# A hand-ordered attention and MLP kernel on one core: a new timetable, the second x tile on another queue, a shorter warm-up

## The chip, the cores and the metric

The kernel runs on one core of a Trainium2 chip. The metric is the device time of one execution in microseconds (us). The engines are named as in the profile: PE (TensorE, matmuls), PEld (its weight loads, which overlap PE), DVE (VectorE), ACT (ScalarE), POOL (GpSimd) and SP (SyncE, which issues nearly all DMAs here).

## The reference

One transformer block over 2048 tokens of width 576: layernorm, attention with 32 heads of 18 in four segments of 512 tokens with a running memory between segments, a residual, layernorm, an MLP with 4608 hidden units and tanh gelu, a residual.

```python
for s in range(N):                       # N = 4 segments of L = 512
    logits = einsum('bhqd,bhkd->bhqk', qs, ks) * scale + mask     # causal inside the segment
    a_dot = einsum('bhqk,bhkd->bhqd', softmax(logits), vs)
    pq = phi(qs)                         # phi(t) = t + 1 if t > 0 else exp(t)
    a_mem = einsum('bhld,bhde->bhle', pq, M) / (einsum('bhld,bhd->bhl', pq, z)[..., None] + 1e-06)
    outs.append(g * a_mem + (1.0 - g) * a_dot)     # g = sigmoid(beta), one per head
    pk = phi(ks); M = M + einsum('bhld,bhle->bhde', pk, vs); z = z + pk.sum over l
h = x + concat(outs) @ wo                # q, k, v = layernorm(x) @ wq, wk, wv
h2 = h + gelu(layernorm(h) @ w1 + b1) @ w2 + b2
```

## The kernel before

The work is cut into some 1840 small steps (`Op`), each on one engine. Each has a tag and a name: `X` is layernorm of x (`stats`, `rstd`, `apply`) with its transposes (`TX`), `P` the projections, `A` attention, `M` the memory's update, `B` output projection, residual and second layernorm, `C` the MLP's first matmul (`F1`) with its evictions (`copy`) and gelu, `D` the second (`F2`) with the last addition (`oadd`). The digit is the segment; in segment 0 a second digit tells its halves or tiles apart. A step's number counts from 0: `A01mask` has four.

The order is written out by hand in `TIMETABLE`: for each step the engine (letters `p a d g s` for PE, ACT, DVE, POOL, SP) and its place among all steps. `Graph.add` looks a step up there, and `Graph.schedule` sorts the steps by place and, with costs of its own, picks the buffer of each. Each engine then runs its steps in that order; between engines, semaphores make a step wait for its inputs and buffers. So a place moves a step past others of its engine, never ahead of its data. SP's order is the order in which DMAs are issued, and a DMA that has to wait holds up those behind it.

The start. `warm_up` issues matmuls on zeros (`warm`): four, four, then two, then X00's first transposes, then three. The first 128 rows of x come in two pieces, `dma.0` on SP's queue and `x0b` on ACT's; the second 128 rows are `x1`, on ACT's queue behind `x0b`. Next on SP stand the two halves of the k weights; then x's fourth tile, the q weights, x's third tile, held until x's first piece has landed (`gate`), and the v weights. In segment 0 the first two tiles are projected by `proj2` (ten matmuls of 288 columns each for k and for q, P00Pk and P00Pq), the rest by `proj_pair`, in two steps (`P`, `R`, between which a `pass` changes banks) or fused in one. q and k rows go to DRAM (`qkst`) and come back transposed (`A0flip`, `A1flip` and so on). The head gates come from beta, a small DMA (`dma.4`) behind P00's `qkst`; `gates.0` on ACT turns it into an exponential, ahead of the first exponential of the scores (`A00exp.0`).

Attention runs by steps: scores on PE (`st0`, `st`), `exp` on ACT over 128x2048, a causal `mask` on DVE (a product with `tri`) or POOL (an affine select), the product with v on PE (`val`), then `valT`, `rec`, `comb` and `oT` on DVE or POOL; for later segments also the memory's part (`eg`, `rg`, `pq`, `mem`, `memT`, `memfin`). The output projection of segment 0 is B00 and B01 (rows 0 to 255), B02 and B03. PE fills its time with the projections of the next segment and with F1 and F2 of the one before. w1 comes in nine groups per segment through four buffers (`C00dma` and so on), w2 in six chunks that stay (`W2dma`); the last three chunks lie where the buffers of q and k rows were (`to_w2`).

Of the kernel before, what the change touches and what calls it, by code (L numbers as in the profile page):

```python
# [25 lines left out]
    "A00exp": "a 91 124",  # L26
    "A00mask": "g101 d125 g133 g164",
    "A00st0": "p 80 109",
    "A01comb": "d172 g197 d225 g214",
    "A01exp": "a 134 136 161 153",  # L30
    "A01mask": "g145 d147 g182 d195",
    "A01oT": "d 198 240 245 234 246",
    "A01rec": "d 168 186 224 212",
    "A01st0": "p 129 132 155 143",
    "A01swap": "g241 d242",
    "A01val": "p 151 201",
    "A01valT": "d 157 158 211 210",
    "A02comb": "g 317 392",
    "A02exp": "a 191 228 207 266 272 283 312",
    "A02mask": "g219 g254 g267 d337",  # L40
    "A02rec": "d 288 369",
    "A02st0": "p 187 222 204 239 271 282 301",
    "A02val": "p 280 281 342 344",
    "A02valT": "d 287 352",
    "A03comb": "g 422 464",
    "A03exp": "a 338 364 350 394 399 420 428",
    "A03mask": "g378 g360 g397 d439",
    "A03oT": "d 381 419 425 485 492",
    "A03rec": "d 417 463",
    "A03st0": "p 332 362 339 379 398 411 427",  # L50
    "A03swap": "a480 g470",
    "A03val": "p 409 412 454 455",
    "A03valT": "d 414 460",
    "A0flip": "s 95 87 128 137 184 189 260 313",
    "A1comb": "g592 d631 g702 g780 g806 g854 d843 g862",
    "A1comb2": "g611 g686 d709 d792 g808 d855 d846 g874",
    "A1eg": "a 462 421 530 677 583 740 719 801",
    "A1exp": "a 458 498 479 579 557 587 613 626 650 674 690 727 713 735 766 750 799 810 817 786",
    "A1flip": "s 410 401 450 575 449 556 688 705",
    "A1mask": "d494 g527 g502 g546 d555 g598 g596 d590 g616 g662 g627 g639 g628 g691 g710 g707 d730 g753 g745 g717 g759 d743 g774 d782 g762 g818 g800 d812 "  # L60
        "g811 g836 g787 g820",
    "A1mem": "p 503 504 629 716 732 815 795 832",
    "A1memT": "d 515 505 630 724 736 824 796 848",
    "A1memfin": "g602 g652 g666 d756 g775 g838 g834 g865",
    "A1oT": "d 822 890 859 876 899",
    "A1pq": "d 477 465 574 703 712 779 755 802",
    "A1rec": "d 584 605 657 741 768 837 797 849",
    "A1rec2": "d 566 606 694 763 784 845 842 853",
    "A1rg": "g 456 407 521 670 497 754 752 788",
    "A1st": "p 457 487 478 570 544 586 600 625 644 665 683 725 711 734 765 749 794 809 816 778",  # L70
    "A1swap": "a 875 885",
    "A1val": "p 563 599 679 726 764 789 826 851",
    "A1valT": "d 565 604 687 729 771 798 839 852",
    "A2comb": "d933 g1009 d1052 d1050 g1120 d1132 g1206 g1219",
    "A2comb2": "d991 g1010 g1061 d1095 d1166 d1142 d1217 g1223",
    "A2eg": "a 823 841 880 1001 971 1040 1129 1060",
    "A2exp": "a 872 840 879 857 893 977 983 967 1020 1028 1042 1059 1071 1049 1083 1107 1119 1148 1128 1161",
    "A2flip": "s 728 807 833 863 888 998 1043 896",
    "A2mask": "g883 d882 g881 g886 g955 g903 d909 g894 g1012 d1014 d1019 g987 g990 d1022 d1029 g1033 g1056 d1077 g1072 d1085 g1087 d1110 g1102 g1084 g1111 "
        "d1133 g1150 d1156 g1186 g1173 g1201 g1195",  # L80
    "A2mem": "p 878 901 994 1045 1003 1118 1160 1162",
    "A2memT": "d 889 902 1008 1062 1016 1125 1168 1167",
    "A2memfin": "g973 g935 g1051 d1074 g1070 g1138 d1216 g1183",
    "A2oT": "d 1090 1105 1204 1227 1236",
    "A2pq": "d 861 884 919 1015 974 1063 1152 1097",
    "A2rec": "d 897 912 1018 1064 1027 1131 1191 1174",
    "A2rec2": "d 929 992 1041 1038 1108 1124 1198 1215",
    "A2rg": "g 844 850 892 941 918 1013 1065 1048",
    "A2st": "p 868 827 877 856 891 976 982 954 1006 1023 1031 1057 1068 1047 1078 1091 1113 1139 1127 1155",
    "A2swap": "a 1225 1229",  # L90
    "A2val": "p 905 970 1032 1036 1096 1117 1158 1211",
    "A2valT": "d 915 972 1034 1037 1098 1123 1169 1214",
    "A3comb": "g1340 g1338 g1405 d1399 g1516 g1474 g1559 g1544",
    "A3comb2": "g1347 g1348 g1408 g1404 g1531 d1493 g1566 g1560",
    "A3eg": "a 1220 1193 1308 1294 1353 1376 1470 1427",
    "A3exp": "a 1185 1210 1222 1298 1232 1328 1342 1309 1371 1356 1416 1394 1420 1436 1446 1457 1468 1479 1487 1499",
    "A3flip": "s 1146 1187 1255 1165 1145 1300 1414 1357",
    "A3mask": "g1271 g1256 g1273 g1251 g1260 g1310 d1272 d1243 d1358 g1362 d1344 g1336 g1329 d1383 d1374 g1364 d1438 g1453 d1437 g1421 g1458 g1443 d1448 "
        "d1447 d1481 d1504 g1502 d1529 d1521 g1488 g1519 g1501",
    "A3mem": "p 1283 1269 1368 1350 1425 1461 1537 1530",  # L100
    "A3memT": "d 1297 1303 1382 1352 1426 1462 1541 1546",
    "A3memfin": "d1343 d1324 g1386 d1389 d1518 d1471 d1558 d1549",
    "A3oT": "d 1372 1429 1569 1568 1575",
    "A3pq": "d 1252 1242 1335 1317 1381 1423 1472 1492",
    "A3rec": "d 1307 1304 1385 1375 1430 1463 1550 1547",
    "A3rec2": "d 1339 1331 1403 1398 1473 1465 1555 1543",
    "A3rg": "g 1208 1240 1320 1314 1261 1387 1415 1486",
    "A3st": "p 1184 1209 1213 1288 1230 1327 1337 1302 1370 1354 1410 1392 1419 1434 1445 1452 1467 1478 1485 1498",
    "A3swap": "d 1570 1565",
    "A3val": "p 1306 1311 1390 1391 1454 1459 1532 1533",  # L110
    "A3valT": "d 1316 1318 1402 1397 1455 1464 1536 1538",
    "B00Po": "p 247",
    "B00Ro": "p 255",
    "B00T": "p 305 328",
    "B00apply": "d 289",
    "B00copy": "d 310 329",
    "B00dma": "s 233 507",
    "B00hadd": "d 259 263",
    "B00pass": "d 250",
    "B00rstd": "g 268",  # L120
    "B00stats": "d 265",
    "B00tail": "d 290",
    "B01Po": "p 256",
    "B01Ro": "p 270",
    "B01T": "p 324 326",
    "B01apply": "d 304",
    "B01copy": "d 325 327",
    "B01dma": "s 235 847",
    "B01hadd": "d 273 276",
    "B01pass": "d 257",  # L130
    "B01rstd": "g 285",
    "B01stats": "d 284",
    "B01tail": "g 316",
    "B02Po": "p 510",
    "B02Ro": "p 519",
    "B02apply": "d 640",
    "B02dma": "s 461 858 673",
    "B02hadd": "d 520 526",
    "B02pass": "d 513",
    "B02rstd": "g 622",  # L140
    "B02stats": "d 541",
    "B02tail": "d 648",
    "B03Po": "p 576",
    "B03Ro": "p 585",
    "B03apply": "d 612",
    "B03dma": "s 501 829 672",
    "B03flip": "s 692 700",
    "B03hadd": "d 591 595",
    "B03pass": "g 578",
    "B03rstd": "g 608",  # L150
    "B03stats": "d 603",
    "B03tail": "d 618",
    "B1Po": "p 906 922 907 916",
    "B1Ro": "p 920 926 927 925",
    "B1apply": "d 948 993 975 958",
    "B1dma": "s 860 949 980 951 1039 999 937 1207 997 910 1092 966",
    "B1flip": "s 1079 1094",
    "B1hadd": "d 921 924 953 968 938 939 928 930",
    "B1pass": "g914 d923 g908 d917",
    "B1rstd": "g 942 986 969 950",  # L160
    "B1stats": "d 931 985 940 932",
    "B1tail": "g957 d995 g984 d963",
    "B2Po": "p 1312 1249 1246 1237",
    "B2Ro": "p 1319 1254 1253 1262",
    "B2apply": "d 1395 1360 1296 1315",
    "B2dma": "s 1321 1365 1400 1205 1359 1366 1163 1287 1346 1284 1599 1388",
    "B2flip": "s 1422 1428",
    "B2hadd": "d 1323 1326 1265 1275 1257 1258 1285 1286",
    "B2pass": "g 1313 1250 1247 1241",
    "B2rstd": "g 1341 1277 1264 1299",  # L170
    "B2stats": "d 1332 1276 1263 1293",
    "B2tail": "d1396 g1361 g1325 g1363",
    "B3Po": "p 1602 1594 1584 1580",
    "B3Ro": "p 1613 1603 1588 1585",
    "B3apply": "d 1675 1677 1637 1652",
    "B3dma": "s 1612 1721 1679 1604 1655 1685 1573 1611 1646 1557 1628 1676",
    "B3flip": "s 1686 1707",
    "B3hadd": "d 1645 1653 1609 1640 1597 1608 1587 1593",
    "B3pass": "d1605 g1601 g1586 g1581",
# [148 lines left out]
    "omg": "g 152",  # L328
    "ones": "a 262 192",
    "tri": "g 55",  # L330
    "warm": "p 1 2 3 23",
    "x0b": "a 8",
    "x1": "a 10",
}
# [1214 lines left out]
```

## Time and profile before

| what | value |
|---|---|
| median of 3 runs | 445.64 us (445.15 to 446.35) |
| the profiled execution | 446.14 us |
| its span | 444.4 us |
| PE busy | 433.7 us |
| ACT busy | 298.1 us |
| DVE busy | 286.3 us |
| POOL busy | 179.5 us |
| DMA | 76.26 MB, mean 172 GB/s |

The span is shorter than the device time of the same execution, because what lies before the first and after the last instruction is left out of it. Busy times of several engines overlap. A matmul's end is modelled, so a busy PE is not a PE at its peak. "Idle before" is time in which an engine had nothing running, with what released it.

### The profile page before, as it was taken

To read this page: it belongs to the slowest core of one execution; us is meant where nothing else is said; L and a number is where in the kernel's file an instruction comes from. 1 tells how busy PE (TensorE), PEld (TensorE's weight loads), DVE (VectorE), ACT (ScalarE), POOL (GpSimd) and SP (SyncE) were. 2 spreads that over 40 slices of the span, in tenths; PEclk is the share of its full clock that TensorE was granted. 3 is DMA by queue.
4 is the path that set the end of the run, shared out by engine and by line. 5 is a ranking of instruction groups with operands and counts; after the bars stand their busy time and mean duration, and the time that the engine had idled before them with its cause. 6 is when DMAs were issued, how large, how long until landed. Compare 5 with 4: busy or idle time off the path is not lost.

```text
span 444.4 us, 12086 instructions
## 1 busy us (share of the span) xinstructions
PE 433.7 (98%) x5089; PEld 277.8 (63%) x5089; DVE 286.3 (64%) x635; ACT 298.1 (67%) x274; POOL 179.5 (40%) x321
## 2 busy tenths in 40 slices
PE   8978999999999999999999999999999999999997
PEld 4755677776677676664444766654457775446775
DVE  4899988899778998968788888642875410000011
ACT  3799889999878898776799976675855001565000
POOL 4587657356735765834132765412111400110000
DMA  7599989997999955893783236913634357550110
GB/s 283 167 217 258 257 251 283 251 287 203 191 270 333 286 118 175 175 236 94 162 228 91 73 90 193 232 20 133 219 97 165 90 142 133 172 177 1 40 41 29
DMA packets 81591, 76.26 MB, mean 172 GB/s; under 512 B 59008, under 2 KB 68864, under 8 KB 81536
## 3 DMA queue, kind: packets, MB, share of 16 engines
q1 hardware_dynamic: 81248, 75.23, 63.5%
q8 instruction: 40, 0.66, 0.6%
q10 hardware_dynamic: 288, 0.25, 0.2%
q14 instruction: 15, 0.12, 0.1%
HBM read 42.30 MB, written 19.20 MB: 138 GB/s over the span
## 4 chain that ended last, share of the span: by engine, by line
PE 87%; DVE 5%; ACT 4%; DMA 2%; issue 1%; ACTq 0%; SPq 0%; DVEq 0%
PE bank L1387 32%; PE bank L1300 24%; PE bank L1337 7%; PE bank L797 6%; PE bank L823 5%; PE bank L1162 4%; PE bank L1188 3%; ACT pt L1166 1%; PE bank L837 1%; DMA x<-in_A_x_dram 1%; DMA beta_bc<-in_A_beta_dram 1%; PE bank L1133 1%; PE bank L1001 1%; ACT pt L1004 1%; DVE pt L1014 1%
## 5 line engine op out<-in xcount | busy, mean ns | idle before, releaser
L1166 ACT ACTIVATE pt<-bank 128x2048 bf16<-128x2048 f32 x60 | 112.6, 1876 | 29.5 <-PE bank L1162 23.2
L1387 PEld LDWEIGHTS <-hT 128*128 128x128 bf16 x1152 | 110.2, 98 | 34.5 <-issue 6.7
L1300 PE MATMUL bank<-xreg,w1g 64*128 64x512 bf16 x972 | 108.0, 376 | 0.0
L1300 PEld LDWEIGHTS <-w1g 64*128 64x128 bf16 x972 | 46.5, 94 | 57.4 <-issue 3.7
L1387 PE MATMUL bank<-w_lo,hT 128*128 128x288 bf16 x576 | 78.1, 286 | 0.0
L1387 PE MATMUL bank<-w,hT 128*128 128x288 bf16 x576 | 77.4, 286 | 0.0
L1399 DVE TENSOR_TENSOR ot<-bank,hc 128x288 bf16<-128x288 f32 x32 | 13.8, 448 | 88.4 <-PE bank L1387 72.5
L1177 POOL TENSOR_SCALAR_AFFINE_SELECT pt<-pt 128x512 bf16<-128x512 bf16 x64 | 45.0, 717 | 42.5 <-ACT pt L1166 41.6
L1305 ACT ACTIVATE hT<-bank,b_col 128x512 bf16<-128x512 f32 x36 | 22.2, 695 | 46.5 <-PE bank L1300 46.3
L1315 DVE TENSOR_SCALAR hT<-bank,b_col 128x512 bf16<-128x512 f32 x46 | 32.8, 741 | 22.1 <-PE bank L1300 20.4
L1373 POOL TENSOR_TENSOR hc<-hc,b_bc 128x576 f32<-128x576 f32 x9 | 11.8, 1320 | 79.0 <-DMA hc<-hd 79.0
L1004 ACT ACTIVATE pt<-bank 128x2048 bf16<-128x2048 f32 x20 | 37.4, 1876 | 4.1 <-PE bank L1001 2.9
L1337 PE MATMUL bank<-xreg,w1g 64*128 64x256 bf16 x648 | 38.1, 269 | 0.0
L823 PE MATMUL bank<-hT,xreg 128*128 128x288 bf16 x250 | 33.8, 286 | 1.7 <-ACT pt L1004 1.0
L1337 PEld LDWEIGHTS <-w1g 64*128 64x128 bf16 x648 | 30.4, 94 | 6.6 <-issue 3.2
L1320 ACT ACTIVATE hT<-hT 128x8192 bf16<-128x8192 bf16 (+2 forms) x6 | 31.8, 5323 | 0.1
L823 PEld LDWEIGHTS <-xreg 128*128 128x128 bf16 x250 | 23.4, 98 | 10.0 <-issue 4.3
L1313 ACT ACTIVATE hT<-bank,b_col 128x512 bf16<-128x512 f32 x26 | 16.9, 685 | 16.1 <-PE bank L1300 15.8
L797 PE MATMUL bank<-hT,xreg 64*128 64x288 bf16 x342 | 24.9, 283 | 0.9 <-DVE qk_pad L647 0.7
L1204 POOL TENSOR_TENSOR t<-t,r 128x288 f32<-128x288 f32 x17 | 13.6, 802 | 29.2 <-DVE r L1201 29.2
L1348 DVE TENSOR_TENSOR hT<-bank,b_col 128x512 bf16<-128x512 f32 x31 | 20.4, 682 | 6.0 <-PE bank L1337 5.8
L1162 PE MATMUL bank<-qk 32*128 32x512 bf16 (+3 forms) x384 | 23.8, 301 | 0.2
(120 smaller groups left out, 592.1 us busy)
## 6 DMA issues: line engine op xcount, KB each, us to landing
w1g<-in_B_w_dram SPq DMA_DIRECT2D x41, 576.0 KB, 5.0
qkd<-qk_pad SPq DMA_DIRECT2D x15, 512.0 KB, 4.8
hd<-h SPq DMA_DIRECT2D x16, 288.0 KB, 3.6
hc<-hd SPq DMA_DIRECT2D x16, 288.0 KB, 3.6
w_lo<-in_B_w_dram SPq DMA_DIRECT2D x3, 864.0 KB, 7.0
w<-in_B_w_dram SPq DMA_DIRECT2D x3, 864.0 KB, 7.5
xb<-in_A_x_dram SPq DMA_DIRECT2D x16, 144.0 KB, 3.1
x2d<-xn SPq DMA_DIRECT2D x14, 160.0 KB, 1.9
```

The lines of the kernel that those rows point to most:

```text
L797: return nc.tensor.matmul(out=cc[hf].t[:, 0:HALF], lhsT=xTb.t[r, k, ts], rhs=wt[r, hf, k, :], start=start, stop=stop, skip_group_check=True)
L823: nc.tensor.matmul(out=cc[hf].t[:, 0:HALF], lhsT=xTb.t[:, k, ts], rhs=wt[:, hf, k, :], start=(k == 0), stop=(k == KT - 1))
L1004: ex = add(ps, {"act": 1.88}, lambda e: nc.scalar.activation(out=pt.t[:], in_=st.t[:], func=ACT.Exp, scale=scale), [sc], pt, [st], table=" ...
L1162: nc.tensor.matmul(out=st.t[:, i, off:off + n_], lhsT=qk[rows, 1, kt * P:(kt + 1) * P], rhs=qk[rows, 0, kt * P:L], start=True, stop=True, ...
L1166: ex = add(ps, {"act": 1.88}, lambda e, st=st, pt=pt: nc.scalar.activation(out=pt.t[:], in_=st.t[:], func=ACT.Exp, scale=scale), [sc], pt, ...
L1177: nc.gpsimd.affine_select(out=blk, in_=blk, pattern=[[0, 4], [1, P]], compare_op=ALU.is_ge, fill=0.0, base=0, channel_multiplier=-1)
L1300: nc.tensor.matmul(out=cc[w].t[:], lhsT=w1.t[rows, k, q, :], rhs=x2T[s].t[rows, k, :], start=(k == 0), stop=(k == ND - 1))
L1305: ready_f[f + w] = [add(pf - 12, {"act": 0.68}, lambda e, f=f, w=w, cc=cc: nc.scalar.activation(out=hT[:, :, f + w, :], in_=cc[w].t[:].rea ...
L1315: nc.vector.tensor_scalar(out=dst, in0=src, scalar1=b, scalar2=None, op0=ALU.add)
L1320: ge = add(2.9, {"act": 0.42 * (f1 - f0) + 0.2}, lambda e, f0=f0, f1=f1: nc.scalar.activation(out=hT[:, :, f0:f1, :], in_=hT[:, :, f0:f1, ...
L1337: nc.tensor.matmul(out=cc[w].t[:, q * 2 * P:(q + 1) * 2 * P], lhsT=w1.t[rows, k, q, :], rhs=x2T[s].t[rows, k, ts], start=(k == 0), stop=(k ...
L1387: nc.tensor.matmul(out=c.t[:, 0:HALF], lhsT=hT[:, tl // 2, f, (tl % 2) * P:(tl % 2 + 1) * P], rhs=w2_c[ch][:, f - ch * WCH, hf * HALF:(hf ...
```

## The change

1. The start: `x1` is issued by SP, second in its queue, and not by ACT behind `x0b`; the k weights follow it. The warm-up's groups of two and three matmuls go; one matmul of 256 columns is added. The first projections no longer name the group of three as something to wait for. X00's `stats` name `x0b` besides `dma.0`.
2. `TIMETABLE` is written anew: 1840 steps with other places, some on other engines.
3. `Graph.schedule` keeps, for DVE and POOL, the stretches of time in which a step holds what both share, and lets a step of the other wait. Its costs set the choice of buffers; they put no instruction into the program.

The code's part of the diff, cut to its core:

```diff
+        d = 0.25 if name == "apply" else 0.14 if name in ("mask", "pq", "comb", "comb2", "memfin", "hc", "fk", "tail", "swap") else 0.0
+        g = 0.15 if name in ("mask", "comb", "comb2", "memfin", "rg", "rk", "hc", "rstd", "eps", "memset", "swap") else 0.0
+        self.rest = (round(cost["dve"] - d, 4) if d and "dve" in cost else 0.0, round(cost["pool"] - g, 4) if g and "pool" in cost else 0.0)
...
+            if e in PORT and op.rest[PORT[e]] > 0:
+                rest, k = op.rest[PORT[e]], PORT[e]
+                g, extra = t0 + c - rest, 0.0
+                for a, z in held[1 - k]:
+                    if g < z and g + rest > a:
+                        if a <= g:
+                            g = z
+                        else:
+                            extra += g + rest - a
...
-        wprev = add(-9, {"pe": 0.5}, lambda e: [nc.tensor.matmul(out=wst.t[:], lhsT=warm[:, 0:P], rhs=warm[:], start=True, stop=True) for _ in range(2)],
-                    [wprev], wst, name="warm")
+        add(-9, {"pe": 0.22}, lambda e: nc.tensor.matmul(out=wst.t[:, 0:2 * P], lhsT=warm[:, 0:P], rhs=warm[:, 0:2 * P], start=True, stop=True),
+            [wprev], wst, name="warm")
...
-        x1 = add(-7.8, {"act": 0.45}, lambda e: nc.scalar.dma_start(out=x0.t[:, 1, :], in_=x[P:2 * P, :]), [x0b], None, [x0], name="x1")
+        x1 = add(-7.8, {"sp": 0.45}, lambda e: nc.sync.dma_start(out=x0.t[:, 1, :], in_=x[P:2 * P, :]), (), None, [x0], size=254e3, name="x1")
+        x1.behind = x0b
...
+        w_ok["k"][0].behind, w_ok["k"][1].behind = x1, w_ok["k"][0]
...
-                elif s == 0:
-                    gr.tag = ""
-                    begun.append(warm_up(3, 0.65, [wprev, xn_ok[0, 0].after[0]], None, [wst]))
...
-                        a = proj2(p0, xT, tl, nm, [xn_ok[s, tl]] + begun, c)
+                        a = proj2(p0, xT, tl, nm, [xn_ok[s, tl]], c)
```

Rows of the timetable that the text speaks of:

```diff
-    "A01comb": "d172 g197 d225 g214",
-    "A01mask": "g145 d147 g182 d195",
-    "A01swap": "g241 d242",
-    "P3qkst": "s 619 731 684 761",
-    "W2dma": "s 517 647 701 790 828 793",
-    "X00dma": "s 37 42 19",
-    "X2stats": "d 135 146 196 200",
-    "dma": "s 4 9 17 44 61 194 261 385",
-    "gate": "g 5",
-    "warm": "p 1 2 3 23",
-    "x1": "a 10",
+    "A01comb": "g 192 203 224 226",
+    "A01mask": "d 130 139 185 181",
+    "A01swap": "g 230 228",
+    "P3qkst": "s 595 784 665 782",
+    "W2dma": "s 570 721 623 815 835 844",
+    "X00dma": "s 18 36 16",
+    "X2stats": "d 143 122 310 328",
+    "dma": "s 0 14 17 46 62 198 220 666",
+    "gate": "d 8",
+    "warm": "p 15 24 103",
+    "x1": "s 5",
```

At the start, PE's order becomes: four warm-up matmuls, X00's first transposes, four more warm-up matmuls, X00's second transposes, then P00Pk twice, the transposes of x's fourth tile, P00Pq twice. SP's order becomes: x's first piece, x's second tile, the first half of k, x's fourth tile, the second half of k, the q weights, x's third tile, segment 1's first x load, the v weights.

More of the change, by code (lines that the diff above doesn't have):

```diff
@@ L411, in schedule @@
         free = dict.fromkeys(ENGINES, 0.8)
-        table, dma, flying, done = {}, 0.0, [], set()
+        table, dma, flying, done = {"act": "exp"}, 0.0, [], set()
+        held = [[(0.0, 0.0)] * 4 for _ in range(2)]
         order = sorted(self.ops, key=lambda o: o.start)
@@ L451, in schedule @@
                 t0 = max(t0, flying[0] if len(flying) > 6 else 0.0)
+            if e in PORT and op.rest[PORT[e]] > 0:
[7 more added lines that the diff above has]
+                            extra += g + rest - a
+                if op.hold >> k & 1:
+                    held[k] = held[k][1:] + [(g, g + rest)]
+                c = g + rest + extra - t0
             op.start, op.end = t0, t0 + c
             free[e] = max(t0, op.end - OVER.get(e, 0.0))
+            op.end += op.lat
             if e == "sp":
@@ L736, in layernorm, with transposes @@
             return add(prio, {"dve": dcost}, apply, [a, b if centred is None else None] + list(extra), dst_buf, [sm, xsrc], name="apply")
-        xnT, xn_ok, applied, begun = {}, {}, [], []
-        def transposes(prio, buf_src, after, dst, dbuf_acq, dbuf_use, nk=KT, name="T", c0=0):
+        xnT, xn_ok, applied = {}, {}, []
+        def transposes(prio, buf_src, after, dst, dbuf_acq, dbuf_use, nk=KT, name="T", c0=0, one=0.06):
             c = Buf(c_s)
@@ L747, in fn @@
                     nc.tensor.transpose(out=ptv[:, k * P:(k + 1) * P], in_=buf_src.t[:, c0 + k * P:c0 + (k + 1) * P], identity=ident[:])
-            a = add(prio, {"pe": 0.06 * nk}, fn, list(after) + [ident_ok], c, [buf_src], name=name)
+            a = add(prio, {"pe": one * nk}, fn, list(after) + [ident_ok], c, [buf_src], name=name)
             return copy(prio - 0.5, 0.70 if nk == KT else 0.60, 0.50 if nk == KT else 0.42, dst, lambda: c.t[:].bitcast(BF16)[:, 0:nk * P].rearrange("p (k q) -> p k q", q=P), [a],
@@ L775, in stage_X @@
                 xn_ok[s, tl] = transposes(prio + 0.1 * tl, xn, [ap], lambda tl=tl: buf.t[:, :, tl * P:(tl + 1) * P],
-                                          buf if tl == 0 else None, [] if tl == 0 else [buf], name="TX")
+                                          buf if tl == 0 else None, [] if tl == 0 else [buf], name="TX", one=0.06 if s or tl else 0.108)
                 if tl:
                     xn_ok[s, tl].after.append(xn_ok[s, 0])
-                elif s == 0:
-                    gr.tag = ""
-                    begun.append(warm_up(3, 0.65, [wprev, xn_ok[0, 0].after[0]], None, [wst]))
             if s in DMA_FLIP_X:
```

8 lines of the change are left out of this document (6 added, 2 removed), and 594 rows, old and new, of the table TIMETABLE.

## The prediction

> **What bounds the kernel now.** I read the page first.
>
> ```profile
> PE 433.7 (98%) x5089; PEld 277.8 (63%) x5089; DVE 286.3 (64%) x635; ACT 298.1 (67%) x274; POOL 179.5 (40%) x321
> PE   8978999999999999999999999999999999999997
> ```
>
> PE (TensorE) is busy 98% of the span, and its only thin slices are the first four and the last. Next, busy time by stage (the columns after the window are its length, then busy us of PE, its weight loads, DVE, ACT, POOL, then clock, DMA share and GB/s).
>
> ```profile
> 0.00:8.00 8.00, 6.05 (x24) 2.64 (x25) 3.32 (x10) 2.64 (x4) 3.22 (x11) 1.00 0.72 251
> 20.00:45.00 25.00, 20.16 (x372) 13.61 (x372) 23.86 (x58) 23.19 (x30) 20.01 (x39) 1.00 1.00 225
> 75.00:112.00 37.00, 36.81 (x555) 26.26 (x553) 33.85 (x81) 36.37 (x34) 19.94 (x38) 1.00 0.98 258
> 200.00:245.00 45.00, 45.00 (x504) 19.76 (x502) 37.46 (x67) 37.13 (x27) 13.68 (x25) 1.00 0.56 142
> ```
>
> The reader is to see that PE has 4.84 us free only in 20 to 45, where DVE (95%) and ACT (93%) are full. From 45 on a gain must be one that PE already carries in, since nothing there lets PE go faster. Pricing each kind of PE step by the lower quartile of its start-to-start times in the trace, 420.5 us are the steps themselves and 18.6 are waits and changes between matmul forms. Of these 7.2 lie before 40 us, and no later stretch of 20 us holds over 1.7. The chain of waits (start, length, what) says what holds PE early.
>
> ```profile
> 1.23 4.84 DMA x<-in_A_x_dram
> 6.09 0.83 DVE ln L719 x2
> 7.19 0.40 DVE xn L733
> 7.63 0.45 PE bank L747 x5
> 8.08 4.92 PE bank L837 x40
> 13.02 0.75 ACT qk_pad L641
> 13.83 0.35 SPq L892
> 14.24 4.33 DMA beta_bc<-in_A_beta_dram
> 18.59 0.11 ACT g_bc L1440
> 18.73 1.87 ACT pt L1004
> ```
>
> So the first exponential (18.73) hangs on x's second tile, which lands at 6.07 among the k weights. Then come four k/q projections, the store of the q/k rows (L892), and beta, which SP issues only behind that store. From 22 to 46 the chain is nearly all DVE.
>
> The profiled execution took 446.14 us, 1.74 beyond its span of 444.40; the median of the three runs is 445.64. I sum changes of the span and take them off the median. About 0.3% (1.34 us) is what a measurement of this kernel can tell from none.
>
> **Part 1: the warm-up.** Thirteen matmuls of 512 columns become eight: two and then three go, and one of 256 columns is put at about 20 us, where PE waits. The five are 0.85 + 0.91 us of PE before 8 us, where it waits for x anyway: worth nothing by itself. What their going does to the rate of PE starts from the timeline of PE.
>
> ```profile
> 1.25 3.59 PE L657 MATMUL bank<-pt 128*128 128x512 bf16 x8 [1.25 <-DVE mhalf L623]
> 4.63 1.06 PE L661 MATMUL bank<-pt 128*128 128x512 bf16 x2
> 5.48 0.74 PE L747 MATMUL bank<-ident,xn 128*128 128x128 bf16 x5
> 6.02 0.91 PE L657 MATMUL bank<-pt 128*128 128x512 bf16 x3
> ```
>
> The eight of the first row start 0.427 us apart; of the last row the first two starts are 0.316 apart and the next 0.217. PE doubled its rate at about 6.2, after 5.0 us of unbroken work (the granted clock of the stage reads 1.00 throughout and does not show it). The changed order is four warm-up matmuls (1.25 to 2.95), the first tile's transposes, which wait for its `apply` (it ends at 4.72 now; a `gate` of under 0.2 us goes ahead of its statistics on DVE: about 4.85), then four more. That opens a hole of 1.9 us. If the rate still doubles at 6.2, the four end at 6.67; at the slow rate at 7.1.
>
> **Part 2: x's second tile.** It moves from ACT's queue to SP's second place. From 3.17 to 6.77 the second piece of x, 160 KB, and both halves of k, 720 KB, landed: 244 KB/us. Ahead of k, x's 160 KB is there at 3.17 + 0.66 = 3.8. DVE then does the first tile's 1.06 + 0.59 and the second's 1.06 + 0.39 back to back, to about 6.3 instead of 7.57, and the transposes wait for the warm-up, not for x. The first projection starts at 6.95 (fast) to 7.65 (slow), against 7.92: 0.3 to 1.0 earlier.
>
> On SP, x's fourth tile, which is held until x's first half has landed (3.0), now stands ahead of the second half of k: its issue goes from 1.71 to about 3.5. It lands at 7.4 by bytes (160 KB more ahead of it) or 8.6 if it takes its present 5.06 from issue. The fast-rate projection needs it at 7.6, the slow at 8.85, so this costs 0 to 1.0 in the fast case and nothing in the slow; I take 0.2. The q weights have the same bytes ahead of them as now (9.55), no change; v moves behind 320 KB of segment 1's x (1.3 us), but its first use moves behind the first scores, near 20.
>
> The store, and so beta, now waits for three projections and five transposes, not four: 30 x 0.123 + 0.28 = 3.97 against 4.92, with the same 0.75 copy (now DVE's). That is 0.95 earlier. If the 5.0 us of unbroken work count anew from the end of the hole, PE is slow until 4.85 + 5.0 = 9.85, and half of the time from 7.65 to there is lost: 1.1. The first exponential: from 0.95 + 0.97 = 1.9 earlier to 0.95 + 0.27 - 1.1 = 0.1 earlier. I take 0.9, near the middle: the hole speaks for the slow end, the eight matmuls that still run for the fast one.
>
> **Part 3: the timetable, 20 to 46.** Until the first output projection (B00's, 45.33 now) DVE loses X2's last two statistics (2.09), two `comb` (0.46, 0.90) and a `swap` (0.19) that go to POOL or later, and seven evictions (0.49, 0.52, 0.51, 0.45, 0.42, 0.45 and one swapped for an equal): 6.5 us. It gains two `mask` of A01, an eviction 0.45, another 0.42, a `fk` 0.74 and 0.3 of small ones. The masks are unpriced in this place; their line gives both bounds.
>
> ```profile
> L1014 DVE TENSOR_TENSOR pt<-pt,tri x5: 639/685/1592, 24.7 to 77.8; 128x1024 bf16<-128x1024 bf16 x5
> ```
>
> The two long ones (1.59, 1.57) each overlap a POOL mask. In the new order POOL has no A01 masks, so 0.64 is nearer. DVE gains 3.2 to 5.0 and sheds 1.5 to 3.3 net. [...]
>
> ACT does not shed. From the first exponential to the fourth of A02 (45.09) it loses one `ones` and two memsets (1.5) and gains three evictions and one `ek` (1.9): +0.3. It idles 1.9 us in that stretch now, waiting for PE and POOL. So ACT, not DVE, sets the pace after the change: 0.9 - 0.3 + half of the 1.9 = 1.5 us earlier at 46 (ends: -0.2 and 3.5).
>
> **Part 4: after 46.** The order of PE keeps the same steps; one projection pair fewer or more in each form, and five more `mem` in four column parts, which take 0.22 to 0.33 in either form: nothing. By the trace's cost of each change of form the new order pays 0.1 to 0.5 more. ACT gets 4.7 us more in all, at 298 of 444 busy, none of it net in 75 to 112, where it has 0.6 to spare; POOL loses 15. Loads: the tightest are w1's sixth group in segment 1, 5.6 us of PE work from buffer to use (8.0 now; landings there take 4.2 to 5.4), and w2's fourth, below. Hidden by PE's own work, zero; uncovered, up to 1 us. Sum: -1.5 + 0.1 = -1.4, so 445.64 - 1.4 = 444.2.
>
> **Rivals.**
> *The slow clock eats it.* The projections run at the slow rate until 9.85, and ACT keeps most of its idle gaps: 0.1 - 0.3 + 0.3 of idle = 0.1 gained: 445.5. For it: the hole, which before has not. Against: PE has little urgent work then. [...]
> *All of it lands*: doubling at 6.2, cheap masks, ACT's gaps closed: 1.9 - 0.3 + 1.4 = 3.0: 442.6.
> *Slower: w2's fourth chunk comes late.* On SP the two last stores of segment 3's q/k rows now stand behind four w1 loads, the last of which waits for the projection C01F1.3. The chunk goes into their buffers, so it waits for their landing. From the end of C01F1.3: 0.8 to the issue, a landing (5.2 to 7.3 now), the chunk's (4.8 to 7.5; the next but one took 9.1). PE reaches D00F2.3 16.9 us of work after C01F1.3, so 10.8 to 15.6 is hidden (slack now about 10). If the landings queue to 9 and 12 us it comes at 21.8, and PE stands 4.9 us: 445.64 + 4.9 - 1.4 = 449.1; at 3 us of stall 447.2. It decides from 16.9.
>
> **How the numbers follow.** Forecast (-1.4, own range -2.3 to -0.6) 0.46, of it 0.26 beyond 1.34; all of it 0.15; the clock 0.22; slower 0.17 (I allow that other waits of a reordered 400 us act like this one). Faster 0.26 + 0.15 = 0.41; same 0.20 + 0.22 = 0.42; slower 0.17. The range 442.6 to 446.8 takes in the second and third cases and the mild end of the slower one.
>
> **What would show it.** Right: the second x tile landing by 4.5; the first exponential at 16.9 to 18.5; A01's masks on DVE near 0.64; B00's projection at about 43.8; PE gapless from there. Wrong: projections 0.24 us apart as late as 9.8; ACT still idling 1.9 us before 46; any PE wait over 0.5 us after 60, above all at D00F2.3 near 150.

## The result, and the profile after

The changed kernel took 444.13 us (median of 22 runs, 442.70 to 446.92), the kernel before 445.99 in as many; the ratio is 0.9964 (95% interval 0.9949 to 0.9980). So it is faster, by 1.6 us (0.9 to 2.3). The forecast had been 444.2, within 442.6 to 446.8.

The profiled execution took 443.06 us, 1.7 beyond its span of 441.4. From its page, the busy totals and PE's slices:

```profile
PE 431.0 (98%) x5100; PEld 276.8 (63%) x5100; DVE 284.6 (64%) x647; ACT 301.1 (68%) x281; POOL 166.8 (38%) x303
PE   7979999999999999999999999999999999999997
```

PE's first and third slices and its last are still thin; the fourth (33 to 44 us) has filled. By stage (length, then busy us of PE, its loads, DVE, ACT, POOL, clock, DMA share, GB/s):

```profile
0.00:8.00 8.00, 5.06 (x20) 2.38 (x21) 4.28 (x15) 2.92 (x5) 4.22 (x15) 1.00 0.66 204
20.00:45.00 25.00, 21.48 (x392) 15.41 (x391) 23.79 (x60) 24.03 (x31) 19.73 (x40) 1.00 1.10 235
75.00:112.00 37.00, 36.77 (x565) 25.58 (x562) 32.48 (x84) 36.47 (x34) 23.12 (x48) 1.00 1.03 256
```

PE does 1.32 us more from 20 to 45, but in that window the changed kernel is also further on in its work. Over the same work, from the first exponential to the fourth of A02, the windows are, before and after:

```profile
18.73:45.09 26.36, 21.34 (x385) 14.28 (x383) 24.83 (x60) 24.46 (x31) 20.10 (x39) 1.00 0.99 229
17.98:43.54 25.56, 22.04 (x395) 15.87 (x396) 23.29 (x58) 24.59 (x32) 19.73 (x40) 1.00 1.05 241
```

The stretch is 0.80 us shorter: DVE does 1.54 us less, and ACT stands for 0.97 us instead of 1.90. The timeline of PE shows the start (start, length, matmuls; in brackets the idle time ahead of them and what ended it):

```profile
1.24 1.89 PE L677 MATMUL bank<-pt 128*128 128x512 bf16 x4 [1.24 <-DVE pt L671]
4.82 0.71 PE L770 MATMUL bank<-ident,xn 128*128 128x128 bf16 x5 [1.69 <-DVE xn L756]
5.33 1.91 PE L677 MATMUL bank<-pt 128*128 128x512 bf16 x4
7.04 0.74 PE L770 MATMUL bank<-ident,xn 128*128 128x128 bf16 x5
7.57 1.01 PE L857 MATMUL bank<-hT,xreg 128*128 128x288 bf16 x5
8.88 1.39 PE L857 MATMUL bank<-hT,xreg 128*128 128x288 bf16 x10 [0.30 <-DMA hT<-in_A_w_dram]
```

The hole of 1.7 us is there, and the 0.30 is the second half of k, which lands only at 8.8. The trace's record of the clock has PE at its full rate from 8.03. The first exponential and A01's masks, from the timeline of ACT and the groups of instructions:

```profile
17.98 1.88 ACT L1024 ACTIVATE pt<-bank 128x2048 bf16<-128x2048 f32 x1
```

```profile
L1034 DVE TENSOR_TENSOR pt<-pt,tri x7: 637/684/1081, 24.1 to 65.5; 128x1024 bf16<-128x1024 bf16 x7
```

How far ahead of the kernel before it stands, in the two profiled executions: 0.75 us at the first exponential (17.98 for 18.73), 1.98 at the first output projection (43.35 for 45.33), 1.87 at A1st.0 (78.31 for 80.18), 2.48 at A1st.8, 2.81 at A2st.0, 3.08 at the end. The first of these figures lies within what executions of one and the same start differ by (part 2, below).

The executions of the changed kernel differ in the mean clock that the throttle granted. In these 22 and the 12 of its second measurement, 19 had 0.999 or 1.00 and a median of 443.5 us, 15 had 0.995 or 0.996 and a median of 445.3. Of 75 executions of the kernel before in the measurements below, 3 were at 0.996. The profile above is one at 1.00, so it shows more gain than the median has.

### The profile page after: what moved, and what is told of

Same layout as the page of the kernel before. It is cut to its first block, busy times and chain, and to the rows that moved or that the text cites. A ratio compares the mean times of both kernels' runs of the same rounds, so it can differ in the third digit from the quotient of the medians.

```text
span 441.4 us, 12114 instructions
## 1 busy us (share of the span) xinstructions
PE 431.0 (98%) x5100; PEld 276.8 (63%) x5100; DVE 284.6 (64%) x647; ACT 301.1 (68%) x281; POOL 166.8 (38%) x303
## 4 chain that ended last, share of the span: by engine, by line
PE 89%; DMA 5%; ACT 3%; SPq 1%; DVE 1%; issue 1%; POOL 0%; ACTq 0%
PE bank L1407 33%; PE bank L1320 24%; PE bank L817 8%; PE bank L1357 7%; PE bank L843 6%; PE bank L1182 4%; PE bank L1208 3%; DMA x<-in_A_x_dram 3%; DMA xreg<-xnd 1%; PE bank L1021 1%; ACT pt L1024 1%; PE bank L1153 1%; ACT hT L1374 1%; PE bank L1053 1%; PE bank L1156 1%
## 5 line engine op out<-in xcount | busy, mean ns | idle before, releaser
L1197 POOL TENSOR_SCALAR_AFFINE_SELECT pt<-pt 128x512 bf16<-128x512 bf16 x57 | 38.9, 693 | 59.3 <-ACT pt L1186 59.3
L1325 ACT ACTIVATE hT<-bank,b_col 128x512 bf16<-128x512 f32 x36 | 22.1, 690 | 46.0 <-PE bank L1320 45.9
L1335 DVE TENSOR_SCALAR hT<-bank,b_col 128x512 bf16<-128x512 f32 x41 | 29.5, 736 | 14.3 <-PE bank L1320 14.3
L1333 ACT ACTIVATE hT<-bank,b_col 128x512 bf16<-128x512 f32 x31 | 19.6, 684 | 16.2 <-PE bank L1320 13.8
L1393 DVE TENSOR_TENSOR hc<-hc,b_bc 128x576 f32<-128x576 f32 x9 | 7.0, 776 | 29.1 <-DMA hc<-hd 29.1
L817 PE MATMUL bank<-hT,xreg 64*128 64x288 bf16 x342 | 23.9, 283 | 0.1
L746 POOL TENSOR_SCALAR ln<-ln 128x1 f32<-128x1 f32 x32 | 9.4, 294 | 35.8 <-DVE ln L743 29.7
## 6 DMA issues: line engine op xcount, KB each, us to landing
xb<-in_A_x_dram SPq DMA_DIRECT2D x16, 144.0 KB, 3.9
```

The source lines that it names most:

```text
L817: return nc.tensor.matmul(out=cc[hf].t[:, 0:HALF], lhsT=xTb.t[r, k, ts], rhs=wt[r, hf, k, :], start=start, stop=stop, skip_group_check=True)
L1197: nc.gpsimd.affine_select(out=blk, in_=blk, pattern=[[0, 4], [1, P]], compare_op=ALU.is_ge, fill=0.0, base=0, channel_multiplier=-1)
L1325: ready_f[f + w] = [add(pf - 12, {"act": 0.68}, lambda e, f=f, w=w, cc=cc: nc.scalar.activation(out=hT[:, :, f + w, :], in_=cc[w].t[:].rea ...
L1335: nc.vector.tensor_scalar(out=dst, in0=src, scalar1=b, scalar2=None, op0=ALU.add)
```

## The experiments

**The changed kernel again** (e0_after), unedited.

> The changed kernel once more, as the measure for the others of this call. Clock theory: its executions fall into two groups, some two thirds at a mean granted clock of 1.00 and 442.7 to 444.5 us, one third at 0.995 to 0.996 and 445.0 to 446.9 us; 0.4% of 443 us is 1.8 us of clock, so PE runs at half rate for 3.5 us longer in the second group, and the doubling falls near 11.5 instead of 8.03. Kernel before: one group, at 1.00 or close to it. Rival (chip or hour): the two groups came from two measuring occasions, and here there is one. Median near 444.1 in both cases.

Measured: 444.92 us (12 runs), ratio 0.9972 (0.9958 to 0.9986). Five runs at 0.999 or 1.00 (443.2 to 446.1), seven at 0.996 (444.2 to 446.1). The two groups belong to the kernel. In this profile the rate doubled at 7.52, k's second half let PE wait until 9.08, and the first exponential came at 18.19.

**PE's hole in the warm-up filled** (e1_hole_filled).

```diff
         wprev = warm_up(4, 1.72, [wprev], [Buf(c_s), Buf(c_s)])
+        wprev = warm_up(4, 1.72, [wprev], [Buf(c_s), Buf(c_s)])
-    "warm": "p 15 24 103",
+    "warm": "p 15 16 24 103",
```

> Four more warm-up matmuls of 512 columns stand ahead of the first tile's transposes and fill PE's hole from 2.95 to 4.66. Clock theory: the rate doubles at about 6.2 as before the change, in every execution; no execution at 0.996; the first projection starts near 6.8 but has to wait for k's second half (8.84), so the first exponential comes only about 0.3 to 0.6 earlier than 17.98; median 442.6 to 443.3. Rival (the groups have nothing to do with the hole): one third of the executions still at 0.996, median 444.1.

Measured: 443.48 us (6 runs), ratio 0.9946 (0.9928 to 0.9964). The rate doubled at 5.84 and the first exponential came at 17.58, as foreseen. But two of six runs were at 0.996, the profiled one among them, so the hole is not the cause of the second group. Its windows show where the clock went:

```profile
22.90:26.30 3.40, 1.52 (x36) 0.93 (x34) 3.37 (x8) 3.40 (x6) 3.23 (x5) 1.00 1.11 238
26.30:29.70 3.40, 3.40 (x20) 1.76 (x18) 2.75 (x8) 2.62 (x3) 3.01 (x9) 0.50 1.10 258
29.70:33.10 3.40, 2.79 (x97) 1.97 (x94) 2.19 (x5) 2.86 (x5) 3.07 (x9) 0.99 1.19 207
```

PE was 45% busy from 22.9 to 26.3 (1.52 of 3.40), and for the next 3.41 us its clock was halved: 20 matmuls fill that window. PE stood there from 24.8 to 26.18 (1.39 us), because two sets of scores held all eight banks of the kernel's `bank` tile until ACT had done A01exp.0 (the profile names ACT's line of `exp` as what ended the 1.39 us). From the first exponential to the first output projection this execution took 26.96 us, against 25.37 in the changed kernel's at 1.00: the fall costs 1.6 us. The changed kernel has the same stand (25.21 to 26.57, 1.36 us). Its emptiest 3.41 us are 42% busy, those of the kernel before 55%. In the profile of e0_after the same stand passed without a fall:

```profile
24.60:28.00 3.40, 1.83 (x26) 1.28 (x25) 3.37 (x8) 3.40 (x3) 3.30 (x4) 1.00 0.88 235
```

In the traces the changes of the clock lie on a grid of 3.413 us (part 1, below). In e0_after's execution it changes at 7.52, and 24.6 is five such windows later: the grid cuts the stand so that PE was busy for 54% of the emptiest window. In e1_hole_filled the window from 22.9 had nearly the whole stand in it.

**The start alone, on the kernel before.** First the shorter warm-up alone, without the single matmul of 256 columns (e6_before_warm), then with x's second tile on SP as well (e7_before_both).

```diff
-        wprev = add(-9, {"pe": 0.5}, lambda e: [nc.tensor.matmul(out=wst.t[:], lhsT=warm[:, 0:P], rhs=warm[:], start=True, stop=True) for _ in range(2)],
-                    [wprev], wst, name="warm")
...
-                    begun.append(warm_up(3, 0.65, [wprev, xn_ok[0, 0].after[0]], None, [wst]))
-    "warm": "p 1 2 3 23",
+    "warm": "p 1 18",
```

```diff
-        x1 = add(-7.8, {"act": 0.45}, lambda e: nc.scalar.dma_start(out=x0.t[:, 1, :], in_=x[P:2 * P, :]), [x0b], None, [x0], name="x1")
+        x1 = add(-7.8, {"sp": 0.45}, lambda e: nc.sync.dma_start(out=x0.t[:, 1, :], in_=x[P:2 * P, :]), (), None, [x0], size=254e3, name="x1")
+        x1.behind = x0b
-    "x1": "a 10",
+    "x1": "s 8.5",
```

> The kernel before with the shorter warm-up alone: two groups of four, the second behind the first tile's transposes (the last single matmul of 256 columns is left out). Clock theory: the hole of 1.8 us makes the doubling late, at 8.0 to 11.5 instead of 6.2, two groups of executions appear as in the changed kernel, and the kernel is 0.3 to 2 us slower than before: 446.3 to 448. Rival: PE has little urgent work there, no second group, within 0.3 us of before.

> The kernel before with the shorter warm-up and with x's second tile on SP's queue ahead of k, but with the timetable of before otherwise. If the gain of the change is its start: first exponential near 18.0, and 0.75 us or more faster than before, 444.2 to 445.3. If it is the timetable after 20 us (it gave 1.23 of the 1.98 us by the first output projection): no more than the 0.75 us at the first exponential, and that partly lost to DVE's stretch from 22 to 46: 445.3 to 446.3, two groups of executions as in the changed kernel.

Measured: 447.85 us, 1.0041 (1.0027 to 1.0056), and 447.75, 1.0039 (1.0025 to 1.0053): both slower than before, by 1.7 to 1.8 us. One of twelve runs was at 0.996, so this is not the second group. With both, the rate doubled at 8.77, five gaps of the first projection were still 0.24 us, and the first exponential came at 19.47, later than in both profiles with the start of before (18.73, and 17.91 in e12_before_mask below). With the warm-up alone it came at 18.33, between those two; its profiled execution is the one at 0.996. Some of the 1.8 us is not in the span at all: these twelve executions took 1.7 to 2.8 us beyond it, those of the kernel before 1.7 to 1.85; why, the traces don't show. In the order of before, the changed start loses.

**The stand of PE shortened** (e9_gap_filled). Sixteen matmuls of the identity into the banks that A01st0.1 fills next.

```diff
+                fill = tag == "A01" and gr.count.get("A01st0") == 0
                 def score(e):
+                    for i in range(16 if fill else 0):
+                        nc.tensor.matmul(out=st.t[:, 3, 0:P], lhsT=ident[:], rhs=ident[:], start=True, stop=True)
```

> The changed kernel with 16 matmuls of 128 columns (identity by identity, 16 x 0.056 = 0.9 us) put just ahead of A01st0.1, into the banks that it fills anyway. PE stands from 25.21 to 26.57 there for banks, and the emptiest 3.41 us of the changed kernel (from 23.2) is 42% busy, against 55% in the kernel before. Theory (a late low window drops the clock): with 67% the clock does not fall back any more, all executions at 0.999 to 1.00, none at 0.996, median 443.0 to 443.6. Rival (the fall has another cause, the warm-up hole for one): half of the executions still at 0.996, median 444.5 to 445. The 0.9 us themselves are hidden, since A01exp.1 starts 1.16 us after A01st0.1 is done; if they are not, all executions lose up to 0.9 us.

Measured: 444.08 us (12 runs, 442.85 to 446.18), ratio 0.9964 (0.9949 to 0.9979). All twelve at 1.00. The timeline of PE has the sixteen ahead of the scores and what is left of the stand:

```profile
24.67 1.05 PE L1019 MATMUL bank<-ident 128*128 128x128 bf16 x16
25.65 0.40 PE L1025 MATMUL bank<-qk 32*128 32x128 bf16 x16
27.07 1.14 PE L843 MATMUL bank<-hT,xreg 128*128 128x288 bf16 x8 [1.01 <-ACT pt L1028]
```

In the four kernels with this edit no run of 36 fell to 0.996. Without it 28 of 64 did, in the measurements that have the changed order there (the changed kernel twice, e1_hole_filled, and e4_x1_act and e13_timetable below). So the stand causes the fall. The median did not come down to the expected 443.0 to 443.6, though: some executions at 1.00 lose time elsewhere. The profiled one lost 1.4 us from 80 to 90. DVE and SP show how:

```profile
82.56 0.45 DVE L758 TENSOR_SCALAR xn<-x,ln 128x640 bf16<-128x640 bf16 x1 [1.62 <-DMA xnd<-xn]
```

```profile
70.06 5.06 SPq L654 DMA_TRANSPOSE qk<-qkd  x2
75.63 0.33 SPq L647 DMA_DIRECT2D w1g<-in_B_w_dram  x1
76.08 1.12 SPq L647 DMA_DIRECT2D xnd<-xn  x2
```

X3apply.2 writes a buffer that the store of X3apply.0's rows must leave first. That store stands on SP behind two transposing loads, which took 5.06 us here and 3.57 in the changed kernel's profile (there the stores go out at 74.54, and DVE waits for nothing). DVE then runs 1.6 us late, and PE waits 0.71 us for its M1macc. Other profiles have this loss in another form, PE itself waiting for the transposed rows of X3. In e1_hole_filled:

```profile
88.91 1.28 PE L844 MATMUL bank<-hT,xreg 128*128 128x288 bf16 x9 [0.61 <-DMA xreg<-xnd]
```

From the first output projection to the end, the four profiles of the order of before took 399.1 to 399.2 us. Of the ten with the changed order six took 398.0 to 398.2, and four 398.7 to 399.4: this one, and e1_hole_filled, e13_timetable and e14_masks_gap, where PE waits 0.6 to 0.9 us for these rows. So late rows of X3 cost 0.7 to 1.4 us in four of ten executions.

**All that pointed forward: stand shortened, hole filled, both halves of k ahead of x's fourth tile** (e10_gap_hole_k). The edits of e1_hole_filled and e9_gap_filled, and

```diff
-    "dma": "s 0 14 17 46 62 198 220 666",
+    "dma": "s 0 14 15 46 62 198 220 666",
```

> The changed kernel with three edits: the 16 matmuls ahead of A01st0.1, four warm-up matmuls more in PE's hole ahead of X00TX.0, and k's second half on SP ahead of x's fourth tile. Theory: no execution at 0.996; the rate doubles near 6; k's second half lands near 7.3 instead of 8.84, the first exponential at 17.2 to 17.6; median 442.0 to 442.8, faster than both kernels. If q's landing (10.6) sets the first exponential, 17.5 and 442.6.

Measured: 442.81 us (6 runs, 442.39 to 444.12), ratio 0.9939 (0.9924 to 0.9953): the lowest median of the kernels measured, with no run at 0.996. Its interval overlaps those of e1_hole_filled and e13_timetable. Its first exponential came at 17.82, no earlier than the hole's 17.58, since x's fourth tile now lands later and X01stats.1, which needs it, stands on DVE ahead of X00copy.1: PE waited 1.19 us for that copy.

**x's second tile back on ACT's queue** (e4_x1_act), in the changed kernel.

```diff
-        x1 = add(-7.8, {"sp": 0.45}, lambda e: nc.sync.dma_start(out=x0.t[:, 1, :], in_=x[P:2 * P, :]), (), None, [x0], size=254e3, name="x1")
-        x1.behind = x0b
+        x1 = add(-7.8, {"act": 0.45}, lambda e: nc.scalar.dma_start(out=x0.t[:, 1, :], in_=x[P:2 * P, :]), [x0b], None, [x0], name="x1")
...
-    "x1": "s 5",
+    "x1": "a 4",
```

> The changed kernel with x's second tile back on ACT's queue behind the first tile's second piece. By the prediction's part 2 the tile lands at 5.5 to 6.1 instead of 3.76 and the transposes of it start at about 7.6 instead of 7.04; the first exponential is 0 to 0.6 later than 17.98, as k's second half lands earlier in exchange (7.6 to 8.8) and q's landing is the same: 0 to 0.6 slower than the changed kernel. If the tile's place carries the change, the whole 0.75 at the first exponential goes and 0.75 of the gain with it.

Measured: 444.49 us (12 runs), ratio 0.9964 (0.9945 to 0.9982); six runs at 1.00 with a median of 442.9, six at 0.996 with 445.6. The second transposes began at 6.91, not 7.6 as expected and no later than with the tile on SP (7.04), since they wait for the second warm-up group. The tile's place is worth nothing that these runs can tell.

**The changed timetable alone** (e13_timetable), with the warm-up of before, x's second tile on ACT's queue and both halves of k first. The rows of the timetable are shown; the code of the start that goes with them is as before the change.

```diff
-    "warm": "p 15 24 103",
+    "warm": "p 15 16 17 24",
-    "x1": "s 5",
+    "x1": "a 4",
-    "dma": "s 0 14 17 46 62 198 220 666",
+    "dma": "s 0 14 15 46 62 198 220 666",
...
```

> The changed timetable alone: the warm-up of before (8 and 2 matmuls ahead of the first tile, 3 behind it), x's second tile on ACT's queue behind the first tile's second piece, both halves of k ahead of x's fourth tile on SP; PE's order from the first projection on, and every other engine's, as changed. If the changed start is worth nothing: median 444.0 to 445.0, with the two groups by clock (about 443.2 at 1.00, 445.4 at 0.996). If the start carries the 0.75 us at the first exponential: 0.75 slower, 444.9 to 445.7.

Measured: 443.65 us (12 runs, 441.94 to 445.69), ratio 0.9947 (0.9932 to 0.9962); seven runs at 0.999 or 1.00 with a median of 443.2, five below with 444.8. The q/k store goes out at 12.63 (13.83 before the change, 13.33 after) and the first exponential comes at 17.32 (18.73 and 17.98); e12_before_mask, a second profile with the start and order of before, has 12.93 and 17.91. So the timetable by itself has the whole gain, and the changed start adds nothing to it that the times show. Whether it takes some back in this order they do not tell: 443.65 against 444.13 and 444.92, with intervals that overlap.

**Two of A01's masks back on POOL**, first alone (e8_masks), then with the stand shortened so that the clock stays up (e14_masks_gap).

```diff
-    "A01mask": "d 130 139 185 181",
+    "A01mask": "g130 d139 g185 d181",
```

> The changed kernel with two of the four A01 masks (A01mask.0 and A01mask.2) back on POOL, as before the change. By the prediction's part 3 a DVE mask beside a POOL mask takes 1.6 instead of 0.64 to 0.69, and POOL's masks some 1.1 to 1.2: 0.3 to 1.5 us slower at the first output projection and at the end. Rival: ACT sets the pace from 18 to 46 and the masks have slack: within 0.3 us of the changed kernel at the first output projection (43.35).

> The changed kernel with two of A01's masks on POOL as in e8_masks, and with the 16 matmuls ahead of A01st0.1 of e9_gap_filled, so that the clock stays at 1.00. In e8_masks the executions at 0.996 took 445.8 to 446.9 and those at 1.00 no less, 445.7 to 448.3, where the changed kernel gains 2 us. If the masks cost only their own time: 0.3 to 0.8 us over e9_gap_filled, 444.4 to 444.9. If an undropped clock brings the stores of X3's tiles late behind the transposing loads (1.62 us of wait in e9_gap_filled): 445.5 to 447, and its profile shows X3apply.2 on DVE waiting for the store, or another wait of that size between 46 and 112.

Measured: 446.47 us (12 runs), 1.0020 (1.0007 to 1.0033), and 446.34 (12 runs, all at 0.999 or 1.00), 1.0002 (0.9987 to 1.0018). Against e9_gap_filled (444.08) the two masks cost 2.3 us by the medians and 1.7 by the ratios to the kernel before (the two were measured on different chips): the whole gain of the change, and more than the 0.3 to 1.5 expected. In the first of them the five runs at 0.996 took no longer than the seven at 1.00 (446.2 and 446.5), so what a fall costs depends on the order around it. POOL, in the second:

```profile
27.56 1.62 POOL L1041 TENSOR_SCALAR_AFFINE_SELECT pt<-pt 128x1024 bf16<-128x1024 bf16 x1 [2.43 <-ACT pt L1028]
29.13 0.95 POOL L643 MEMSET MZ_blk<- 128x1024 bf16 x1
30.03 1.09 POOL L1041 TENSOR_SCALAR_AFFINE_SELECT pt<-pt 128x1024 bf16<-128x1024 bf16 x1
```

and DVE:

```profile
31.81 0.72 DVE L1071 STREAM_TRANSPOSE t<-bank 128x512 f32<-128x512 f32 x1 [1.97 <-PE bank L1057]
```

A01mask.0 takes 1.62 us beside a DVE mask. It stands ahead of A00mask.0 and first waits 2.43 us for A01exp.0, so A00mask.0 starts at 30.03 where it starts at 26.50 in e9_gap_filled. PE's val step needs it, and DVE stands 1.97 us for that. The first output projection comes 27.64 us after the first exponential, against 25.16. X3apply.2 does not wait for a store here; of the waits expected between 46 and 112 the profile has PE's 0.8 us for X3's transposed rows, and the greater part of the cost comes earlier. So most of the cost is POOL's order and not the price of a mask. Part of it is of the edit's own making: the place 130 was chosen for DVE, and on POOL it lies ahead of A00mask.0's 133.

**One of A01's masks on DVE in the kernel before** (e12_before_mask).

```diff
-    "A01mask": "g145 d147 g182 d195",
+    "A01mask": "d145 d147 g182 d195",
```

> The kernel before with one edit: the first of A01's masks on DVE instead of POOL (two DVE masks side by side in that stretch, POOL 1.1 us less). If the engine of the masks by itself carries the gain: 0.5 us or more faster, 445.4 or less. If it pays only together with the rest of the order (combs and statistics off DVE in exchange): within 0.3 us of before, or slower, since DVE is 95% busy there: 445.6 to 446.6.

Measured: 446.58 us (12 runs), 1.0005 (0.9996 to 1.0014): nothing. From the first exponential to the first output projection 26.58 us, before 26.60. In the old order, to take one mask off POOL buys nothing.

**The stores ahead of a transposing load** (e11_store_first), on top of e10_gap_hole_k.

```diff
-    "A1flip": "s 413 416 450 475 593 493 663 727",
+    "A1flip": "s 413 438 450 475 593 493 663 727",
```

> The kernel with the three edits (matmuls ahead of A01st0.1, four warm-up matmuls more, k's second half first) and one more: on SP the second of A1's transposing loads (A1flip.1) stands behind the stores of X3's normalized tiles instead of ahead of them. Theory: in the execution of e9_gap_filled the two transposing loads together took 5.06 us of SP (3.57 in the changed kernel's), the stores behind them came 1.5 us later, X3apply.2 on DVE waited 1.62 us for one, and PE 0.71 and more for DVE; with the stores ahead of one of them no execution has that wait. Median 442.2 to 442.8, no execution over 443.5. Rival: A1st.2 or X3's flips, now later, come late in its place: 443 or more, with a wait of PE between 80 and 95.

Measured: 444.41 us (6 runs, 442.88 to 444.89), ratio 0.9952 (0.9935 to 0.9968), no better. In its profile the stores' wait is gone (X3apply.2 at 81.64 without one), and 80 to 90 costs nothing extra. The loss is at the start, where X01stats.1 waits on DVE for x's fourth tile, which lands at 8.68 (7.46 in e10_gap_hole_k):

```profile
8.70 0.82 DVE L743 BATCH_NORM_STATS2 ln<-x 128x6 f32<-128x288 bf16 x2 [2.77 <-DMA x<-in_A_x_dram]
```

PE waits 2.44 us for the copy behind it, and the first exponential comes at 19.04, 1.2 later than in e10_gap_hole_k, whose start is the same code. How often the tile lands so late, one profile of each doesn't tell.

## Why the prediction was right, point by point

The sum was -1.4 us off the median, and the medians gave -1.86 in the first measurement and -0.92 in the second. But that is a mean of two prices, neither of which the sum had. The executions at 1.00 gain 2.5 us (443.5 against 446.0), where "all of it lands" had 3.0; those at 0.996 gain 0.7 (445.3), where "the slow clock eats it" had 0.1. They came 19 to 15, where I gave that rival 0.22. The median lies between, where the forecast was: the 0.9 that the sum took for the start is not seen in the times, the gain of the order was sized too small, and a fall of the clock that the sum did not have takes the excess back. The mechanism of 20 to 46 was right; that the total came so near is in part luck.

**Part 1.** The hole was nearly as foreseen (1.7 us for 1.9), and the rate doubled between 7.52 and 10.71 in the eight profiles that have it, three of them past the 9.85 given as the slow end (9.99, 10.23, 10.71). Without the hole it was 5.84, 5.30, 5.26, 6.33 and 4.97 in five. The step that failed is "after 5.0 us of unbroken work": the trace's clock changes lie on a grid of 3.413 us (in e1_hole_filled the rate rises at 5.84, falls at 26.32, six times 3.413 later, and rises at 29.73) whose phase differs by execution (8.03, 7.52 and 9.99 with the same start). Laid over PE's busy time, the rate doubled after the first grid window that was 0.81 or more busy, never after one of 0.51 to 0.76 with the hole in it: in the changed kernel's profile the window from 1.20 was 0.55 busy and that from 4.62 0.94; in that of e9_gap_filled the one from 3.16 was 0.52 and the one from 6.57 full.

**Part 2.** The tile landed at 3.8 and the transposes waited for the warm-up, both as written. k's second half landed at 8.84 in the changed kernel, 0.24 beyond the bound of 8.6, and cost 0.30 (0.2 taken) there, 0.91 in the second profile. q landed at 10.64 and not at 9.55 unchanged, which cost nothing. The first exponential came 0.75 earlier in the two profiled executions, of 0.9 taken, but that is no measure of the term. Five profiles with the changed start have it at 17.98, 18.19, 18.47, 18.64 and 18.94, and e12_before_mask, whose start is that of before, has x's second tile at 5.08 in place of 6.07 and the exponential at 17.91:

```profile
1.21 3.87 DMA x<-in_A_x_dram
17.91 1.87 ACT pt L1004
```

So executions of one start differ by about as much as the whole term, the prediction's 6.07 was a late landing (ACT's queue brings the tile at 5.08 to 5.54 in the four other profiles that have it there), and the 0.9 is not shown. Of the 0.95 for a store that waits for three projections in place of four, e13_timetable has the store 1.20 earlier than the first profile of before and 0.30 earlier than e12_before_mask: its sign fits, its size stays open.

**Part 3.** A01's masks were taken at 0.64 each by their nearest rows and took 0.64 to 0.69. Of what DVE and POOL share, as `Graph.schedule` has it, the runs show masks that run side by side: 1.59 and 1.57 us for DVE's beside POOL's before the change, 1.62 for POOL's beside DVE's in e14_masks_gap, where the shortest take 0.64 and 1.10. From the first exponential to the first output projection DVE sheds 1.98 us (25.07 to 23.09), within the 1.5 to 3.3, and ACT is the fuller engine after the change, as foreseen. Up to the fourth exponential of A02 it has 0.13 us more work (0.3 taken), and of its 1.9 us of idle time about half goes (0.97 left; 0.77 to 1.11 in the five profiles without a fall that have the changed order with these masks on DVE, 1.89 to 1.92 in the three of the order of before without one). That is 0.80 us where the sum had 0.6. To the first output projection the gain is 1.23: in these profiles the way there from the first exponential takes 25.2 to 25.5 us, for 26.6. The sum had no term for the 0.4 behind the exponential. Nor did it have POOL, whose lighter queue was named only in part 4, as 15 us less with no effect: e14_masks_gap puts two masks back on it, ACT idles 3.08 us, and the whole gain is gone. The rival's place was wrong too: not the hole at the start but the stand of PE at 25 us takes the clock down, a step that the sum did not have. With a fall the stretch takes 26.7 to 27.0 us in three profiles, and all that the order gains there is gone. The clock fell after grid windows of 3.41 us that were 40 to 45% busy (four profiles) and once after two of 59%, while windows of 54 to 60% passed in three others. One of 40 to 45% was enough in all four profiles that have one. Where the limit lies is open: two windows of 59% fell in e6_before_warm and passed in e7_before_both.

**Part 4.** "+0.1 after 46" had the wrong sign: from the first output projection to the end the changed order took 398.0 to 398.2 us in six profiles, the order of before 399.1 to 399.2 in four, so 1.1 was gained. Which of the moved steps bring it no run here shows. In four further profiles 0.7 to 1.4 us of it was lost again to X3's late rows.

**"Slower: w2's fourth chunk."** It did not happen: from C01F1.3's end (130.49) its issue came 8.3 us later (138.83) and its landing 5.2 after that (144.0), 13.5 in all, within the 10.8 to 15.6 given and under the 16.9 from which it decides. PE reached D00F2.3 at 147.21 without a wait. The late load of this kind was another, the store of X3's rows on SP behind transposing loads, allowed for among "other waits"; it cost 0.7 to 1.4 us where it came.

## What to carry to other kernels

Price an order of steps on the queue of every engine that a step is taken off, also of the one that the page calls idle: POOL was busy 40% of the span, yet one mask that waits at its head held up DVE, one of the two fullest engines of that stretch, by 2 us. Look for windows of a few us in which the matmul engine is under half busy, not just for long gaps, and compare the two kernels there (here the clock fell after windows of 3.41 us that were 40 to 45% busy, in four profiles); a few filler matmuls into banks that are about to be overwritten kept the clock up in 36 of 36 runs, though alone they left the median where it was (a ratio of 0.9964 with and without). Do not read a term of under 1 us off one profile of each kernel: here one and the same start gave first exponentials up to 1 us apart. And when a median moves by half a per cent, read the single executions by their clock before the reasons: here one kernel had two prices, 1.8 us apart.

## What the runs showed of the hardware

The granted clock fell for one grid window, 3.413 us at half rate, and was full again after it, in all five profiles at 0.996 (e1_hole_filled, shown above at 0.50 from 26.3 to 29.7, e4_x1_act, e6_before_warm, e8_masks and e13_timetable). The same program has both outcomes (19 of the changed kernel's 34 executions without a fall, 15 with one). That it depends on how the grid lies over the stand of PE fits the profiles: four with a grid window 40 to 45% busy fell, the two of the changed kernel itself, with 54 and 60%, did not; no one program was profiled in both states. And the time that SP took to issue the same two transposing loads varied from execution to execution (3.57, 4.30 and 5.06 us for one pair in three profiles of the same order); behind the longest the next stores went out 1.5 us later than behind the shortest (76.08 and 74.54).
